# A recurrent attention block with streamed weights: new homes for two residual tiles, a larger GpSimd descriptor ring, and a smaller kept part of one output unit

## The chip, the cores and the metric

The kernel runs on one core of one Trainium2 chip. The metric is the device time of that core in microseconds (us), the median of the runs shown.

## The reference, cut to what matters

Two blocks are computed from one layer-normed input and added to it. Block B is a dense layer with GELU (1024 to 3584 to 1024). Block A is attention that passes over the sequence in 64 segments of 32 tokens and carries 8 memory rows from each segment to the next, so its segments can't be computed side by side:

```python
xn = _layernorm(x)                                   # x: 1 x 2048 x 1024
mem = mem0                                           # 8 rows
for s in range(64):
    h = concatenate([mem, xn[:, 32*s:32*s+32]])      # 40 rows
    q, k, v = h @ Wq, h @ Wk, h @ Wv                 # 32 heads of 128
    p = softmax(where(mask, q k^T * scale, -1e9))
    o = (p v) @ Wo                                   # 40 x 1024
    mem = o[:, :8]; outs.append(o[:, 8:])
return x + concatenate(outs) + B(xn)
```

## The kernel before

**Two parts.** The first part (about 440 us) computes the layer norm, block B and the residual R = x + B(xn), and writes to DRAM what the loop reads again: for each segment a row of `hr_d` that holds the transposed input (columns 0 to 255) and the residual (columns 256 to 511), and for the rows called left a row of `hrL_d` in the same form. The second part is the loop over 64 segments, `for s in range(NSEG)`, written out in full: there is no loop on the chip. All instructions of an engine run in the order in which the code makes them (`manual_schedule`); a tracker of the written and read regions of each tile adds the semaphore waits.

**Segments in groups of four.** `g, i4 = divmod(s, GRP)`: `i4` is 0 for the first segment of a group, 3 for the fourth. Of the 32 tokens of a segment, 24 are handled in it with the 8 memory rows; the other 8, the left ones, are collected over four segments and pushed through the products once for a group. Which pass carries left rows depends on `i4`: the output product does where `i4 == 1` (and in the last segment), flagged `left_o`. There the sum tile `psX` has 512 columns, 256 of the segment and 256 of the left rows.

**Weight units.** The four weight matrices are 64 units of 128 x 2048 bf16 (512 KB), used in each segment in the order K, Q, K, Q (half of the heads each), V, V, O. 46 units stay in SBUF; 18 are read anew in every segment (`PLACED` marks them with S). Of those, two are kept in PSUM banks and are copied into a slot by VectorE (L242); the others come from DRAM copies `Wc_...` over SyncE's queue (L244, L246) into one of six slots (`STREAM_BUFS`). `unit_done` (L669) runs after each unit's product: it starts the next stream into the slot that has become free, and takes one or two entries of the list `small`, which are DMAs on GpSimd's queue. One streamed output unit, `HALF`, is special: the first of its two 128 x 1024 parts stays in SBUF in `half_home` (L137), and only the second is streamed (L243); `o_product` takes the kept part from `half_home` (L899).

**One segment.** Passes K0, Q0, K1, Q1, V0, V1 multiply the input `hr_home` (line L709) with the units. `scores(0)` runs after the first unit of Q1: products into `mixed`, then the exp of ScalarE from `mixed` into the attention-weight tile `pr_all` (L823), then the masking on VectorE (L828). `sums(0)`, after the last unit of Q1, adds up `pr_all` (L836, L842), makes the reciprocals on ScalarE (L847, L850), and writes the scaled weights to `pd_main` and `pd_left` (L857, L861). `scores(1)` and `sums(1)` do the same in V1. `values` multiplies `pd_main` and `pd_left` with V (L876, L882) and stores to `d_oL` or `b_oL` (L890). Then the O pass (L902) sums 16 units into `psX`, one of three PSUM banks that the passes share. At its end the first rows become the new memory: ScalarE copies `psX` (L997), `put_mem` transposes it on TensorE (L277), and VectorE casts it into `hr_home` (L281), which has been loaded with the next segment's input meanwhile (L254, issued after V1). Last, VectorE adds the residual to `psX` in place of the residual tile (L1012), the bank is let go (L1018), and GpSimd's queue stores the tile.

**Homes of the residual.** The residual of the segment is loaded at the first unit of the O pass by `load_res` (L964) into `pr_all`, which the exps of the segment have finished with. In a `left_o` segment the left residual is loaded after unit 7 of the O pass into the first 256 columns of `pd_main` (L991, L992). The next segment's exp (L823) writes to `pr_all` again.

**Stores.** They go by GpSimd's queue. Where `i4` is 0 or 3, four stores of 24 rows go from `pr_all` straight to the output (L1051). Where `left_o` holds, four stores go to `outL_d` (L1017) and from there, by `small`, to the output (L1042). Where `i4 == 2`, the tile goes to `outM_d` (L1044) and from there by `small` in two pieces of 12 tokens to the output (L1048). In segments 1 to 4 `small` also holds the transfers of the last residual rows from `R_n` to `hr_d` and `hrL_d` (L446).

**The lowest SBUF bytes.** The area of GpSimd's DMA descriptors is cut to `SCRATCH` = 352 bytes per partition (L130), and `SMALL` = 3744 bytes behind it hold `half_home`, `pr_all`, `pd_main`, `hr_home` and some constants at fixed addresses. `ident`, the identity matrix of the first part's transposes, lies in `pr_all`.

The softmax here doesn't subtract the row's maximum and nothing guards it: scores larger than these inputs give would overflow.

## Time and profile before

| | us |
|---|---|
| median of the three runs shown | 1982.02 (1969.82 to 1986.70) |
| the profiled execution, its own time | 1987.94 |
| its span, first to last instruction | 1986.2 |
| TensorE busy (matmuls) | 1747.1, 88% of the span |
| VectorE, ScalarE, GpSimd busy | 918.9, 638.5, 286.6 |
| DMA: bytes moved, mean rate over the span | 610.03 MB, 307 GB/s |
| granted TensorE clock, mean | 0.983 |

All shares and waits are those of the one profiled execution. A busy TensorE means that matmuls are in its pipeline, not that it works at its peak. A row of the waits reads: engine, tile and line that waited, what ended the wait, us in total, how often, the longest. A row of the timeline reads: start in us from the span's start, us, engine, line, operation, what it writes and reads, how many such instructions were merged, and in brackets the idle time before it with what ended it. "issue" there stands for a wait that the profile shows no semaphore for. A row of sums over stretches reads: the stretch, its length, busy us of PE, PEld, DVE, ACT and POOL with the number of instructions, the granted clock, the mean busy share of the 16 DMA engines, and GB/s.

### The profile page before, as it was taken

Reading aid. Unit: us, or ns where it says so; the run is one execution under the profiler, and the core shown is the slowest. Engines: PE = TensorE matmul, PEld = TensorE weight load, DVE = VectorE, ACT = ScalarE, POOL = GpSimd, SP = SyncE. Lnnn points to the kernel's source line nnn. Section 1 sums busy time; section 2 is a strip of 40 time slices with the busy share of each in tenths; the row PEclk is TensorE's granted clock in tenths of the full one; section 3 lists DMA queues with packets and bytes.
Section 4 is the critical chain, followed back from the end, with each engine's and each line's share of the span. In section 5 each row is a group of like instructions: output and inputs, shape, how many; then the busy total and the mean of one; then the engine's idle time right before and its main releaser. Section 6 shows DMA issues by size and latency. Waiting matters only on the chain. (4 is left out here: it accounts for less than half of the span.)

```text
span 1986.2 us, 73232 instructions
## 1 busy us (share of the span) xinstructions
PE 1747.1 (88%) x32275; PEld 938.2 (47%) x32275; DVE 918.9 (46%) x2222; ACT 638.5 (32%) x1356; POOL 286.6 (14%) x554
## 2 busy tenths in 40 slices
PE   7999999987878888998988888888888989888887
PEld 3444444444444454555544545454444445444443
DVE  6656565323434444444444444444444444444443
ACT  6343434212222332333333233233232333223232
POOL 0000000002331111111111121111111111111111
PEclk9999999989899999999999999999999999999999
DMA  9821212888889999999999999999999999899997
GB/s 329 243 55 42 56 41 56 305 321 308 290 317 342 349 360 339 373 368 373 347 376 356 349 374 341 353 362 363 347 356 341 386 357 375 326 358 356 339 359 294
DMA packets 220283, 610.03 MB, mean 307 GB/s; under 512 B 47675, under 2 KB 65771, under 8 KB 219948
## 3 DMA queue, kind: packets, MB, share of 16 engines
q1 hardware_dynamic: 199036, 585.18, 80.0%
q0 software_dynamic: 16832, 17.52, 2.8%
q8 instruction: 253, 4.15, 0.8%
q10 hardware_dynamic: 4096, 2.64, 0.4%
q14 instruction: 66, 0.54, 0.1%
HBM read 591.00 MB, written 30.21 MB: 313 GB/s over the span
## 5 line engine op out<-in xcount | busy, mean ns | idle before, releaser
L709 PE MATMUL acc<-u,hr_home 128*32 128x512 bf16 x11520 | 791.8, 387 | 60.7 <-DVE hr_home L281 21.3
L709 PEld LDWEIGHTS <-hr_home 128*32 128x32 bf16 x12288 | 345.6, 98 | 360.3 <-issue 62.4
L709 PE MATMUL acc<-u,hrL 128*32 128x512 bf16 x2880 | 256.4, 389 | 22.4 <-issue 8.2
L498 PE MATMUL ps<-u 128*128 128x512 bf16 x896 | 195.6, 381 | 2.6 <-ACT u L382 2.6
L902 PE MATMUL acc<-u,d_oL 128*32 128x256 bf16 (+1 forms) x3330 | 173.2, 290 | 18.8 <-DMA u<-Wc_O 15.9
L242 DVE COPY u<-kept 128x1024 bf16<-128x1024 bf16 x254 | 163.0, 683 | 16.0 <-PE acc L902 7.2
L902 PEld LDWEIGHTS <-b_oL 128*32 128x32 bf16 (+1 forms) x3552 | 108.9, 99 | 86.4 <-issue 50.0
L902 PE MATMUL acc<-u,b_oL 128*32 128x256 bf16 (+1 forms) x1776 | 119.0, 291 | 31.9 <-DMA u<-Wc_O 24.3
L547 PE MATMUL ps<-u 128*128 128x512 bf16 x672 | 147.0, 379 | 0.0
L498 PEld LDWEIGHTS <-u 128*128 128x128 bf16 x896 | 88.0, 98 | 108.9 <-issue 3.4
L902 PEld LDWEIGHTS <-d_oL 128*32 128x32 bf16 (+1 forms) x3552 | 104.4, 98 | 68.5 <-issue 28.2
L857 DVE TENSOR_TENSOR pd_main<-pr_all,mixed 128x320 bf16<-128x320 bf16 x128 | 61.9, 484 | 143.6 <-ACT mixed L850 141.5
L709 PEld LDWEIGHTS <-hrL 128*32 128x32 bf16 x3072 | 85.4, 97 | 86.5 <-issue 24.5
L767 DVE STREAM_TRANSPOSE b_oL<-b_oL 128x512 bf16<-128x512 bf16 x128 | 90.5, 707 | 63.4 <-ACT b_oL L753 63.4
L828 DVE TENSOR_TENSOR pr_all<-pr_all,mixed 128x96 bf16<-128x96 bf16 (+1 forms) x256 | 37.9, 189 | 166.1 <-ACT pr_all L823 166.1
L753 ACT CAST kT<-acc 128x512 bf16<-128x512 f32 x64 | 37.5, 585 | 237.2 <-PE acc L709 237.2
L902 PE MATMUL acc<-W_O,b_oL 128*32 128x256 bf16 (+1 forms) x1776 | 106.2, 289 | 6.1 <-issue 6.1
L753 ACT CAST b_oL<-acc 128x512 bf16<-128x512 f32 x128 | 75.2, 587 | 109.9 <-PE acc L709 109.9
L254 POOL DMA_DIRECT2D hr_home<-hr_d x58 | 33.1, 571 | 488.8 <-PE acc L709 394.0
L547 PEld LDWEIGHTS <-u 128*128 128x128 bf16 x672 | 65.3, 98 | 77.4 <-DVE g_u L514 0.4
L281 DVE CAST hr_home<-mixed 128x64 bf16<-128x64 f32 x63 | 14.1, 225 | 186.6 <-PE mixed L277 120.1
L997 ACT CAST d_oL<-acc 128x256 bf16<-128x256 f32 (+1 forms) x63 | 26.8, 426 | 221.3 <-PE acc L902 221.3
(132 smaller groups left out, 2120.7 us busy)
## 6 DMA issues: line engine op xcount, KB each, us to landing
u<-Wc_K SPq DMA_DIRECT2D x256, 512.0 KB
u<-Wc_V SPq DMA_DIRECT2D x256, 512.0 KB
u<-Wc_O SPq DMA_DIRECT2D x256, 512.0 KB
u<-Wc_Q SPq DMA_DIRECT2D x192, 512.0 KB
u<-Wc_O SPq DMA_DIRECT2D x64, 256.0 KB
u<-in_B_w_dram SPq DMA_DIRECT2D x14, 512.0 KB
u<-in_A_Wq_dram SPq DMA_DIRECT2D x13, 512.0 KB
u<-in_A_Wv_dram SPq DMA_DIRECT2D x12, 512.0 KB
```

The lines of the kernel that those rows point to most:

```text
L242: nc.vector.tensor_copy(out=t[:, c0:c0 + 1024], in_=bank)
L254: eng.dma_start(out=hr_home[:, :], in_=hr_d[s, :, 0:256])
L281: nc.vector.tensor_copy(out=hT[:, :, NX:SEG].rearrange("p (j c) t -> p j c t", c=nc_), in_=psM.rearrange("p c j t -> p j c t"),)
L498: nc.tensor.matmul(ps[:, :].rearrange("p (s t) -> p s t", t=SEG), lhsT=w1_sb[fb // 14 * 8 + kt][:, (fb % 14) * P:(fb % 14 + 1) * P], rhs=x ...
L547: nc.tensor.matmul(ps[:, :], lhsT=gts[fc // 4][:, fc % 4, t * P:(t + 1) * P], rhs=w2_sb[fc // 2][:, fc % 2, cs], start=(fc == 0), stop=(fc ...
L709: nc.tensor.matmul(o, lhsT=lhs[:, i, :], rhs=m, start=(i == seq[0]), stop=(i == seq[-1]), tile_position=(0, 32 * j),)
L753: cp(out=out, in_=ps.rearrange("p (h e) -> p h e", e=32))
L767: nc.vector.transpose(out=home, in_=home)
L828: nc.vector.tensor_tensor(out=p, in0=p, in1=m[:, None, :].to_broadcast([P, 4, n]), op=ALU.min)
L857: nc.vector.tensor_tensor(out=pdA.rearrange("p c b q -> p b c q"), in0=prA[:, None, :, :].to_broadcast([P, 2, 4, 40]), in1=dd, op=ALU.mult,)
L902: nc.tensor.matmul(acc[r:r + n // 8, 0:n], lhsT=lhs[:, 4 * (i % 4) + 2 * u + k, :], rhs=w_k[:, n * jq:n * jq + n], start=(unit == O_UNITS[ ...
L997: nc.scalar.copy(out=o_sb[:, 0:no, :], in_=psX[:, 0:32 * no].rearrange("p (h e) -> p h e", e=32))
```

## The change

- The descriptor area grows from 352 to 512 bytes per partition; the area of small tiles behind it shrinks by as much.
- Of the special output unit, now called `PART`, 512 of its 2048 columns stay in SBUF (`part_home`, the first quarter of the old `half_home`), and 1536 are streamed in each segment instead of 1024.
- The freed half of `half_home` holds two tiles of 256 columns: `res_home` for the segment's residual, and `pr_all`. The place of the old `pr_all` goes to `hr_home`; `pd_left` moves from a pool to a fixed address; `ident` lies in `pd_main`.
- `load_res` fills `res_home` instead of `pr_all`. The left residual is loaded into `pr_all`, after unit 1 of the O pass instead of after unit 7 into `pd_main`.
- In a `left_o` segment, the left residual is added and stored first, and then the segment's own.
- Where `i4 == 2`, the output leaves `outM_d` in one DMA of 24 tokens instead of two of 12.

```diff
-SCRATCH = 352
-SMALL = 3744
+SCRATCH = 512
+SMALL = 3584
...
-AT_BANKS, AT_HALF = 5, 2
+AT_BANKS, AT_PART = 5, 2
+PART_COLS = 512
...
     half_home = nc.alloc_sbuf_tensor_at("half_home", [P, DM], BF16, offset=SCRATCH)
-    pr_all = nc.alloc_sbuf_tensor_at("pr_all", [P, 256], BF16, offset=SCRATCH + 2048)
+    hr_home = nc.alloc_sbuf_tensor_at("hr_home", [P, 256], BF16, offset=SCRATCH + 2048)
     pd_main = nc.alloc_sbuf_tensor_at("pd_main", [P, 320], BF16, offset=SCRATCH + 2560)
-    hr_home = nc.alloc_sbuf_tensor_at("hr_home", [P, 256], BF16, offset=SCRATCH + 3200)
-    small_consts = nc.alloc_sbuf_tensor_at("small_consts", [P, 16], BF16, offset=SCRATCH + 3712)
+    pd_left = nc.alloc_sbuf_tensor_at("pd_left", [P, 128], BF16, offset=SCRATCH + 3200)
+    small_consts = nc.alloc_sbuf_tensor_at("small_consts", [P, 16], BF16, offset=SCRATCH + 3456)
+
+    part_home, res_home, pr_all = half_home[:, 0:PART_COLS], half_home[:, 512:768], half_home[:, 768:1024]
...
-        elif unit == HALF:
-            nc.sync.dma_start(out=t[:, 1024:2048], in_=copies[unit])
+        elif unit == PART:
+            nc.sync.dma_start(out=t[:, PART_COLS:], in_=copies[unit])
...
-                    w_k = half_home if unit == HALF and k == 0 else t[:, 1024 * k:1024 * k + 1024]
                     for jq in range(DM // n):
-                        r = n // 8 * jq
+                        r, c0 = n // 8 * jq, DM * k + n * jq
+                        w_t = part_home if unit == PART and c0 < PART_COLS else t
...
-                            rhs=w_k[:, n * jq:n * jq + n],
+                            rhs=w_t[:, c0:c0 + n],
...
             def load_res():
-                st["res"] = pr_all
+                st["res"] = res_home
...
-                if n == 7 and left_o:
-                    st["resL"] = pd_main[:, 0:256]
+                if n == 1 and left_o:
+                    st["resL"] = pr_all
                     nc.gpsimd.dma_start(out=st["resL"][:, :], in_=hrL_d[og, :, 256:512])
...
-            for w, r in enumerate(tiles):
+            for w, r in reversed(list(enumerate(tiles))):
...
-                for t in (slice(0, NX // 2), slice(NX // 2, NX)):
-                    small.append(lambda o=o[:, t, :], r=r[:, t, :]: nc.gpsimd.dma_start(out=o, in_=r))
+                small.append(lambda o=o, r=r: nc.gpsimd.dma_start(out=o, in_=r))
```

## The prediction, made before the changed kernel ran

> **What bounds the kernel now.** I read four views in this order: the slices of the page, the waits of TensorE, the GpSimd queue and a timeline of one segment, and sums over stretches.

> Slices first. From slice 9 of 40 on (about 447 us) the recurrent loop runs, and the DMA engines are 8 or 9 tenths busy until the end. They carry the streamed weights.

> ```profile
> DMA  9821212888889999999999999999999999899997
> GB/s 329 243 55 42 56 41 56 305 321 308 290 317 342 349 360 339 373 368 373 347 376 356 349 374 341 353 362 363 347 356 341 386 357 375 326 358 356 339 359 294
> ```

> Sums over stretches (us, busy of PE, PEld, DVE, ACT, POOL, granted clock, DMA share, GB/s) say how near the loop is to that limit:

> ```profile
> 549.00:580.00 31.00, 22.56 (x514) 12.89 (x517) 10.68 (x25) 7.35 (x17) 14.76 (x27) 0.89 0.78 280
> 604.00:1960.00 1356.00, 1176.05 (x26960) 663.16 (x26952) 604.97 (x1438) 419.67 (x969) 224.39 (x418) 0.99 0.96 357
> 1380.80:1408.60 27.80, 24.89 (x606) 15.31 (x600) 12.24 (x29) 7.66 (x19) 3.00 (x5) 1.00 1.01 385
> 1408.60:1431.00 22.40, 18.23 (x448) 10.11 (x449) 10.65 (x25) 6.98 (x16) 3.15 (x6) 1.00 0.85 297
> ```

> Over the steady part the DMA engines are 0.96 busy at 357 GB/s, so 0.04 x 1356 = 54 us are idle DMA time. The same view laid over single segments (from one memory update at L281 to the next, averaged) puts the idle part where TensorE stalls: share 0.90 in first segments of a group of four, 0.97 in third, 0.99 in second and fourth. The loop is thus nearly stream-bound, with holes that stalls of TensorE tear: a stalled TensorE frees no slot, and with six slots the stream soon has nowhere to write.

> The waits of TensorE (us, times, longest):

> ```profile
> PE acc L902 <- DMA u<-Wc_O: 40.3, 58, 2.6
> PE mixed L836 <- DVE pr_all L828: 30.8, 22, 7.3
> PE acc L709 <- DVE hr_home L281: 21.3, 16, 3.2
> PE acc L709 <- DVE pd_main L1012: 19.9, 13, 4.8
> PE acc L709 <- DVE pr_all L1012: 4.0, 5, 1.3
> ```

> The first is the stream itself. The other four, 76.0 us, have causes that the change touches. The GpSimd queue and the timeline at the end of a fourth segment show the causes:

> ```profile
> 1386.48 0.54 POOL L1044 DMA_DIRECT2D outM_d<-pr_all  x1 [6.17 <-DVE pr_all L1012]
> 1391.78 0.66 POOL L1048 DMA_DIRECT2D out_dram<-outM_d  x1 [4.76 <-DMA outM_d<-pr_all]
> 1399.07 0.64 POOL L1048 DMA_DIRECT2D out_dram<-outM_d  x1 [6.63 <-issue]
> 1404.77 0.60 POOL L254 DMA_DIRECT2D hr_home<-hr_d  x1 [5.06 <-DVE b_oL L890]
> 1405.37 0.56 POOL L964 DMA_DIRECT2D pr_all<-hr_d  x1
> 1408.56 0.22 DVE L281 CAST hr_home<-mixed 128x64 bf16<-128x64 f32 x1 [2.95 <-DMA hr_home<-hr_d]
> 1411.39 2.77 PE L709 MATMUL acc<-u,hr_home 128*32 128x512 bf16 x48 [0.64 <-DVE pr_all L1012]
> 1418.56 0.36 ACT L823 ACTIVATE pr_all<-mixed 128x224 bf16<-128x224 f32 x1 [2.62 <-DMA out_dram<-pr_all]
> 1419.30 0.25 PE L836 MATMUL mixed<-pr_all,small_consts 128*32 128x160 bf16 x4 [1.87 <-DVE pr_all L828]
> ```

> The second out piece waits 6.63 us on nothing that has a semaphore, and starts 0.3 us after the first has landed (1398.77); the load of hr_home starts 0.3 us after the second has landed (1404.47). V's products ended near 1400.4, so the load is some 4 us late, with it the memory update, the residual, its stores, and the next exp, which writes into pr_all while the stores still read it.

> [...]

> **The change part by part.** Sums are against the profiled execution, 1987.94 us (span 1986.2 and 1.7 around it); the median shown is 5.9 us lower.

> *Own residual home (L962).* The exp of L823 no longer waits for stores of the main residual: its waits for out_dram<-pr_all and outM_d<-pr_all, 38.2 + 7.3 us, end, and with them TensorE's 30.8 us at L836. The timeline has 13.3 of these at 533, 564 and 590 us (4.6, 7.3, 1.4), 17.5 later. The load of L964 also stops waiting for L861 (37.5 us, 38 times: about 1.0 us earlier each), worth the 4.0 us of L1012 pr_all. Next late is the exp's own input, mixed L817.

> *Left residual in pr_all, loaded at unit 1 (L991) and added first (L1011).* Today it waits for pd_main, which the value products read to unit 6, and L1012 waits 41.2 us in 16 segments for it to land; TensorE loses 19.9 us because the bank psX stays taken. At unit 1 it waits only for L861, done before, is issued some 4 us earlier and lands (4.9 us) as the output products end. All 19.9 us go. It adds a wait: in the 16 segments that follow, the exp waits for the two stores of the left half. In the group at 1362, L281 is at 1362.16, these stores would land near 1368 by the 4.3 and 4.7 us of their like, and the exp is due near 1368.7. Behind the exp stand the rest of ACT's work and L836. Bounds: 0, and 16 x 0.7 = 11 us should they land as late as the slowest 7 us of this queue; I take 1.

> [...] the second piece's issue and its wait go (91.8 us in 16, off the path). A load still has to wait for that piece [...]. Its landing is not in the trace: between 7.0 us (the first piece; latency hides the rows) and 11.4 (two of 5.7). From 1391.8 that frees the load at 1399 to 1403.5, against 1404.8, and V's end at 1400.4 is what it then waits for. Of the 21.3 us at L281 the timeline has 17.8 at these ends; I take 15 (bounds 5 and 17.8).

> *A quarter kept (L54, L243, L899).* 128 KB more per segment, 64 times 0.131 MB = 8.4 MB. At a full stream, 357/0.96 = 371 GB/s, that is 0.353 us x 64 = 22.6 us. The product reads its weights from another address; instruction and shape counts don't change. The copy in the first part is two DMAs for one, in slices with DMA 1 to 2 tenths busy: nothing. ident and pd_left move house: nothing.

> *The sum.* Removable stalls: before 604 us, 13.3 + 4.8 (pd_main, at 497) + 0.9 = 19; after, 17.5 + 15 + 15.1 + 3.1 - 1 = 50. They don't all become time, because TensorE would only meet the stream sooner. Before 604 the DMA share in the three slow segments is 0.78 to 0.84, so I let 75% through: 14. After, the ceiling is the 54 us of idle DMA; the holes lie where the stalls are, which speaks for most, and the stream's wait (40.3 at L902, in the same segments) for less: 65%, 33 (choice; bounds 20% and 100%: 10 and 50). The added bytes at 0.96 of 22.6: 22. Net -14 - 33 + 22 = -25: 1963 for the profiled execution, **1957** from the median.

> **The rivals.** *The stream takes it back* (slower than before). Slots are freed sooner, but the stream has no more to give: 20% of the 50 us come through, 10, early ones 4 [...], and the bytes cost all 22.6: +9, 1991; at no conversion 2005. For it: 0.96 busy, and TensorE waits for Wc_O just where the added quarter is streamed. Against it: a share of 0.85 at 297 GB/s in the segment after the late load. It decides once less than 22.6/69 = 33% of the stalls convert. *The single piece holds the queue as long as two did*: 15 less to gain, 10 of it time: -15, 1967; [...] against it: 5.7 us is mostly latency, as these pieces land in 2.2 when the DMA is quiet. *Everything converts*: 19 + 50 - 22 = -47, 1935, as second and fourth segments run today at 0.99.

> **How the numbers follow.** Chances: forecast 0.43, stream takes it back 0.22, single piece 0.18, everything converts 0.17. About 1% is what a measurement of this kernel can tell from no change (its runs shown span 0.85%): 1962 and 2002. Faster by more: most of the forecast and all of the last, 0.53; slower by more: the far end of the stream rival, 0.10; the rest 0.37. The range, 1930 to 1997, leaves out 0.1 on either side.

> **What would show it.** Right: no wait of L823 on an out store; hr_home's load in every fourth segment at V's end; one out piece of about 7 to 9 us; L1012 not waiting for hrL_d; DMA share near 0.98 in first segments; L836, L281 and L1012 gone from TensorE's waits, Wc_O's wait grown by less than they were. Wrong: Wc_O's and the other streams' waits grown by as much as the others shrank at a share that stays 0.96; exp waiting for outL_d<-pr_all in third segments.

## The result: 1911.98 us, and the profile after

The changed kernel takes 1911.98 us (median of four runs, 1909.69 to 1917.95). The kernel before, measured beside it, takes 1984.36 us (four runs, 1969.82 to 1989.31). The ratio is 0.965, with a 95% interval from 0.960 to 0.971. So the change is 72 us faster. The forecast was 25 us faster, 1957 us, in a range from 1930 to 1997: the sign was right, the size was not, and the measured time lies 18 us below the range.

Everything below compares one profiled execution of each kernel: spans of 1986.2 and 1911.5 us, 74.7 us apart. Line numbers of the loop are 5 higher in the changed kernel (L281 is now L286, L709 is L714, L836 is L841, L902 is L907, L1012 is L1017), those of the last output stores 4 higher (L1048 is L1052). The tracker names `res_home` and `pr_all` by the tile that they are parts of, `half_home`.

**The slices of the page**, after. Columns are 40 equal parts of the span: the granted TensorE clock in tenths, the DMA share in tenths, GB/s.

```profile
PEclk9999999998999999999999999999999999999999
DMA  9921212598999999999999999999999999999998
GB/s 339 259 53 42 57 43 53 208 330 301 392 378 388 373 381 384 384 367 396 373 389 376 363 377 362 353 376 382 376 393 383 386 364 379 356 388 365 380 373 318
```

The DMA row was 8 or 9 through the loop and is now 9 from the eleventh slice to the last but one, with 353 to 396 GB/s. And there is a row that the prediction did not show. Before, it had a second dip inside the loop:

```profile
PEclk9999999989899999999999999999999999999999
```

The digit 8 that both kernels have is a stretch of 10.2 us at half clock, from 432 us before and from 431 after, where the first part passes into the loop. The other 8 of before, in the slice from 497 to 546 us, is gone.

**Sums over stretches.** The columns are the stretch, its length, busy us of PE, PEld, DVE, ACT and POOL, the granted clock, the DMA share, GB/s. Both ends of a stretch are starts of the cast of the new memory (L281, L286), so that the same segments are compared: first segments 1 to 4, called early, then the 58 after them, called later. Before:

```profile
468.10:579.40 111.30, 88.47 (x1908) 47.67 (x1900) 42.28 (x101) 29.41 (x68) 41.81 (x76) 0.91 0.85 306
579.40:1957.70 1378.30, 1195.46 (x27348) 672.86 (x27344) 613.66 (x1459) 427.24 (x986) 227.61 (x424) 0.99 0.96 357
```

After:

```profile
466.81:558.54 91.73, 81.53 (x1908) 48.00 (x1900) 42.70 (x101) 29.45 (x68) 41.38 (x75) 1.00 1.00 383
558.54:1884.40 1325.86, 1186.46 (x27348) 677.87 (x27344) 615.61 (x1459) 426.87 (x986) 219.27 (x410) 1.00 0.99 377
```

The four early segments give 19.6 us, the 58 later ones 52.4 us; the rest of the 74.7 us, 2.7, lies outside. Two readings of these rows matter:

- TensorE executes the same 27348 matmuls in the later stretch and is busy 9.0 us less; in the early stretch, with 1908 matmuls in both, 6.9 us less. A wait that goes away cannot do that. A higher clock can, and the rows show one: 0.91 and 0.99 before, 1.00 after.
- The stream moves more bytes in less time. Later stretch: 492 MB at 357 GB/s, then 499 MB at 377.

**The waits of TensorE**, after, over the whole span (us, times, longest):

```profile
PE acc L714 <- issue: 30.6, 36, 2.0
PE acc L907 <- DMA u<-Wc_O: 28.4, 57, 1.6
PE acc L907 <- issue: 20.6, 25, 2.6
PE mixed L816 <- DVE b_oL L772: 19.1, 31, 0.7
...
PE acc L714 <- DVE hr_home L286: 2.4, 6, 0.7
...
PE acc L714 <- DVE half_home L1017: 0.2, 1, 0.2
```

The four waits that the prediction set out to remove were 76.0 us. L836 (now L841) on the masking and L1012 (now L1017) on `pd_main` are no longer in the list (two issue waits, 2.6 us together, are left at L841), the one on `hr_home` is 2.4 us, the one on the residual 0.2 us. The stream's own wait, Wc_O, did not grow; it fell from 40.3 to 28.4 us. What grew is "issue", the wait without a semaphore.

**What TensorE's issue waits are.** The page lists a DMA queue of the kind "instruction":

```profile
q8 instruction: 252, 4.13, 0.8%
```

These are 252 packets of 16 KB. In the later stretch TensorE has 40 issue waits before and 72 after. Each of them ends 1.2 to 1.6 us after the end of a packet of this queue; only 6 to 7% of all matmuls start at such a distance. And when TensorE's instructions are counted off in blocks of 256, all these waits come at the same place of a block, to within two instructions. I read them as waits for its next block of instructions; the traces show the packets and the places, not what is in them. One such wait cuts a run of 12 products in two:

```profile
1653.07 0.81 PE L714 MATMUL acc<-u,hrL 128*32 128x512 bf16 x9
1655.91 0.40 PE L714 MATMUL acc<-u,hrL 128*32 128x512 bf16 x3 [2.03 <-issue]
```

In the later stretch these waits grow from 32.3 to 62.1 us, while those on the stream's DMAs fall from 44.5 to 35.6. On that reading, the changed kernel waits longer for instructions than for the stream.

**GpSimd's queue** in one group, after (start, us, engine, line, what it writes and reads, in brackets the idle time before it and what ended it):

```profile
1338.26 0.55 POOL L1049 DMA_DIRECT2D outM_d<-half_home  x1 [6.75 <-DVE half_home L1017]
1343.55 0.71 POOL L1052 DMA_DIRECT2D out_dram<-outM_d  x1 [4.74 <-DMA outM_d<-half_home]
1353.44 0.57 POOL L259 DMA_DIRECT2D hr_home<-hr_d  x1 [9.19 <-PE acc L714]
1354.01 0.54 POOL L969 DMA_DIRECT2D half_home<-hr_d  x1
1360.45 2.05 POOL L1055 DMA_DIRECT2D out_dram<-half_home  x4 [5.90 <-DVE half_home L1017]
```

One out piece, and the load of `hr_home` behind it is released by TensorE (the end of V); before, the second piece had waited 6.63 us at the issue ahead of it. The whole queue: 56 of the 58 loads at L259 are released by the products at L714, the other two by those at L907.

### The profile page after: what moved, and what is told of

The parts are those of the page before. It is cut to its first block, busy times and chain, and to the rows that moved or that the text cites. A ratio compares the mean times of both kernels' runs of the same rounds, so it can differ in the third digit from the quotient of the medians.

```text
span 1911.5 us, 72993 instructions
## 1 busy us (share of the span) xinstructions
PE 1728.4 (90%) x32255; PEld 943.5 (49%) x32275; DVE 921.1 (48%) x2222; ACT 638.3 (33%) x1356; POOL 277.3 (15%) x538
## 3 DMA queue, kind: packets, MB, share of 16 engines
q10 hardware_dynamic: 4096, 2.64, 0.5%
## 4 chain that ended last, share of the span: by engine, by line
PE 67%; DMA 20%; DVE 6%; issue 4%; ACT 3%; POOL 0%; DVEq 0%; ACTq 0%; POOLq 0%; SPq 0%
PE acc L714 32%; DMA u<-Wc_O 14%; PE ps L503 10%; PE acc L907 10%; PE ps L552 8%; DMA u<-Wc_Q 2%; PE ps L587 2%; PE acc L881 2%; ACT mixed L855 1%; DVE b_oL L772 1%; PE mixed L816 1%; DMA hr_home<-hr_d 1%; DVE pd_main L862 1%; PE pT L587 1%; ACT mixed L852 1%
## 5 line engine op out<-in xcount | busy, mean ns | idle before, releaser
L714 PE MATMUL acc<-u,hr_home 128*32 128x512 bf16 x11520 | 777.8, 381 | 27.4 <-issue 12.3
L714 PEld LDWEIGHTS <-hr_home 128*32 128x32 bf16 x12288 | 350.5, 97 | 309.6 <-issue 62.1
L714 PE MATMUL acc<-u,hrL 128*32 128x512 bf16 x2880 | 256.3, 380 | 22.2 <-issue 14.3
L907 PE MATMUL acc<-u,d_oL 128*32 128x256 bf16 x3441 | 181.5, 292 | 21.0 <-DMA u<-Wc_O 12.5
L907 PEld LDWEIGHTS <-b_oL 128*32 128x32 bf16 (+1 forms) x3552 | 109.4, 98 | 84.8 <-issue 49.5
L907 PEld LDWEIGHTS <-d_oL 128*32 128x32 bf16 (+1 forms) x3552 | 107.5, 99 | 74.1 <-issue 37.0
L907 PE MATMUL acc<-u,b_oL 128*32 128x256 bf16 (+1 forms) x1776 | 118.7, 290 | 26.8 <-DMA u<-Wc_O 15.9
L862 DVE TENSOR_TENSOR pd_main<-half_home,mixed 128x320 bf16<-128x320 bf16 x128 | 62.5, 488 | 155.5 <-ACT mixed L855 144.8
L714 PEld LDWEIGHTS <-hrL 128*32 128x32 bf16 x3072 | 86.8, 96 | 81.5 <-issue 25.3
L907 PE MATMUL acc<-W_O,b_oL 128*32 128x256 bf16 (+1 forms) x1776 | 106.4, 289 | 8.1 <-issue 8.1
L259 POOL DMA_DIRECT2D hr_home<-hr_d x58 | 32.7, 564 | 554.2 <-PE acc L714 546.9
L758 ACT CAST kT<-acc 128x512 bf16<-128x512 f32 x64 | 37.5, 586 | 220.2 <-PE acc L714 220.2
L855 ACT ACTIVATE mixed<-mixed,small_consts 128x160 f32<-128x160 f32 x256 | 94.2, 368 | 8.4
L511 ACT ACTIVATE g_xb<-ps,b1col 128x512 bf16<-128x512 f32 x112 | 76.9, 687 | 60.1 <-PE ps L503 59.0
```

Of the source, the lines that this page charges most:

```text
L511: nc.scalar.activation(out=xb[:, :], in_=ps[:, :], func=ACT.Identity, bias=b1col[:, fb:fb + 1], scale=1.0)
L714: nc.tensor.matmul(o, lhsT=lhs[:, i, :], rhs=m, start=(i == seq[0]), stop=(i == seq[-1]), tile_position=(0, 32 * j),)
L758: cp(out=out, in_=ps.rearrange("p (h e) -> p h e", e=32))
L855: nc.scalar.activation(out=mixed[:, 160 * b:160 * b + 160], in_=mixed[:, 0:160], func=ACT.Exp, scale=-1.0, bias=off[:, b:b + 1],)
L862: nc.vector.tensor_tensor(out=pdA.rearrange("p c b q -> p b c q"), in0=prA[:, None, :, :].to_broadcast([P, 2, 4, 40]), in1=dd, op=ALU.mult,)
L907: nc.tensor.matmul(acc[r:r + n // 8, 0:n], lhsT=lhs[:, 4 * (i % 4) + 2 * u + k, :], rhs=w_t[:, c0:c0 + n], start=(unit == O_UNITS[0] and k ...
```

## The experiments: two set out, none measured; and what the two traces tell apart

No variant of either kernel was measured for this study. So no run separates the homes from the descriptors, and none prices the added bytes alone. Two experiments with expectations on record were to divide the change into its parts; they are shown because they say which question is left open, and how it can be settled. Their expectations were written after the two traces had been read. Two more were set out with expectations and not measured either: the added bytes alone in the kernel before, and the changed kernel with 128 KB less per segment. In the two expectations below, theory A holds that waits and the half clock behind them both turn into time; theory C is the forecast's: waits alone, at two thirds.

*The larger descriptor area and the single piece alone*, with the changed kernel's bytes, against the changed kernel:

```diff
-                st["res"] = res_home
+                st["res"] = pr_all
...
-                if n == 1 and left_o:
-                    st["resL"] = pr_all
+                if n == 7 and left_o:
+                    st["resL"] = pd_main[:, 0:256]
...
-            for w, r in reversed(list(enumerate(tiles))):
+            for w, r in enumerate(tiles):
```

> [...] the homes of the residual as before. Theory A (waits, and half clock behind them, go with the homes and with the queue): 1952 to 1972 us, ratio 0.984 to 0.994; the waits on L836 and pd_main stay. Theory C (waits alone, at two thirds, as forecast): about 1942 us is reached only with the homes, here no gain over 1 per cent.

Measured: nothing; no chip ran it.

*The homes alone*, with the changed kernel's bytes and a small descriptor area (320 bytes; before had 352), against the changed kernel:

```diff
-SCRATCH = 512
-SMALL = 3584
+SCRATCH = 320
+SMALL = 3776
...
-                small.append(lambda o=o, r=r: nc.gpsimd.dma_start(out=o, in_=r))
+                for t in (slice(0, NX // 2), slice(NX // 2, NX)):
+                    small.append(lambda o=o[:, t, :], r=r[:, t, :]: nc.gpsimd.dma_start(out=o, in_=r))
```

> Edit: only the two homes of the change, with its bytes; the out pieces stay two [...]. Theory A: 1937 to 1947 us, ratio 0.976 to 0.981, with fewer than 8 half-clock stretches in the loop; hr_home's waits stay. Theory C: 1950 to 1965 us.

Measured: nothing; no chip ran it. Theory A and theory C thus stand untested by a run, and the division between the parts, which both give in numbers, is not shown.

What follows is argued from two traces; where it says "behind" it means order in time, not a shown cause. Two comparisons inside the traces come nearest to an experiment.

**First comparison: the four segments of a group.** The change touches different waits in each place of a group, while the added quarter is streamed in all of them. Averages over the later stretch, us per segment (14 or 15 segments of a place), from cast to cast; a wait counts where it ends. "Named" is the sum of TensorE's waits on an instruction of another engine. Each cell has before, then after.

| place | length | named waits | waits on DMAs | issue waits | TensorE busy |
|---|---|---|---|---|---|
| first | 23.60, 22.98 | 2.49, 0.18 | 1.03, 0.26 | 0.45, 2.15 | 20.55, 20.32 |
| second | 24.08, 24.12 | 1.88, 0.74 | 0.23, 0.35 | 0.30, 0.90 | 21.73, 22.05 |
| third | 22.67, 21.60 | 1.82, 0.83 | 1.63, 1.63 | 0.34, 0.29 | 18.71, 18.73 |
| fourth | 24.76, 22.74 | 0.82, 0.82 | 0.15, 0.16 | 1.17, 1.00 | 21.51, 20.73 |

The fourth and the first have to be read together, since the late load of `hr_home` lengthens the end of the fourth, and the wait for it ends in the first. Three readings:

- Fourth and first: 2.31 us of named waits go, 0.76 of DMA waits go too, 1.53 of issue waits come, TensorE is busy 1.01 us less, and the pair is 2.64 us shorter.
- Second: 1.14 us of named waits go, 0.60 of issue waits and 0.12 of DMA waits come, TensorE is busy 0.32 us longer, and the length does not change. This place ran at a DMA share of 0.99 before and does so after. The rival "the stream takes it back" gives the right length here, but TensorE's own waits on the stream hardly grow. Whether the full DMA engines or the issue waits hold the length is not shown.
- Third: 0.99 us of named waits go (those on `pd_main` were 1.01), the others stay, the segment is 1.07 us shorter. All of it converts, and TensorE's waits show no sign of the added bytes.

Times the number of segments: 14 x 2.64 = 37 from the pair, 15 x 1.07 = 16 from the third, nothing from the second: 53, which is the later stretch's gain. The homes' and the descriptors' waits mix in the pair (0.59 us of L836 and 1.27 of `hr_home` in the first place), so this does not divide the gain between the two parts of the change.

**Second comparison: the clock, stretch by stretch.** The trace's clock record has 14 stretches inside before's loop at half the granted clock, 58 us together: three of 6.8 us among the early segments, eleven of 3.4 us later. After has three of 3.4 us, 10 us together. Two of before's, in the columns of the sums above:

```profile
497.00:504.00 7.00, 6.15 (x60) 2.28 (x64) 3.06 (x6) 0.58 (x1) 3.75 (x8) 0.52 0.44 123
562.00:569.00 7.00, 4.03 (x48) 1.56 (x52) 3.50 (x9) 1.90 (x5) 5.97 (x11) 0.53 0.25 76
```

In the first of them, TensorE is busy 6.15 of 7 us and gets through 60 matmuls; after has 160 in 6.14 busy us at about the same time of the loop:

```profile
497.00:504.00 7.00, 6.14 (x160) 3.35 (x156) 4.45 (x13) 3.34 (x9) 4.33 (x8) 1.00 1.00 387
```

(The mixes of matmuls differ, so 60 to 160 is no ratio of clocks.) Each of before's stretches was laid beside the waits ahead of it. Nine start in or just behind a wait that the change removes or shortens: at 497 and 610 us behind `pd_main` (4.8 and 2.2 us), at 531, 562 and 1705 behind L836 (4.6, 7.3, 2.7), at 753, 1125, 1221 and 1507 behind `hr_home` (3.2, 2.1, 2.5, 2.9). The other five stand behind one wait on issue or several shorter waits, most of them on issue or on the stream. The timeline of TensorE at 1507 us of before (start, us, operation, idle time before it in brackets) shows one:

```profile
1503.59 0.82 PE L709 MATMUL acc<-u,hrL 128*32 128x512 bf16 x12
1507.26 0.62 PE L709 MATMUL acc<-u,hr_home 128*32 128x512 bf16 x4 [2.86 <-DVE hr_home L281]
1507.66 1.50 PE L709 MATMUL acc<-low,hr_home 128*32 128x512 bf16 x12
1508.94 3.42 PE L709 MATMUL acc<-u,hr_home 128*32 128x512 bf16 x44
```

Ahead of the wait, 12 products take 0.82 us; behind it, 12 products of the same shape and line take 1.50 us, in the stretch recorded at half clock. The end of the stretch at 562 us shows the way back, in the same view:

```profile
567.03 0.64 PE L709 MATMUL acc<-u,hr_home 128*32 128x512 bf16 x4
567.45 0.64 PE L709 MATMUL acc<-u,hrL 128*32 128x512 bf16 x4
...
569.12 0.39 PE L709 MATMUL acc<-u,hr_home 128*32 128x512 bf16 x4
569.34 0.38 PE L709 MATMUL acc<-u,hrL 128*32 128x512 bf16 x4
```

Four products begin every 0.43 us up to 568.3 us, and every 0.22 us from 568.7 us, just behind the end of the half in the clock record (568.63). Nothing is waited for between them, so this is the clock and not a stall. The length of a wait does not tell which waits half clock follows: one of 2.11 us at 1122 us was followed by it, and one of 2.60 at 674 us was not.

A better sign can be worked out from the clock record. In each trace all its changes inside the loop lie a whole number of 3.413 us apart (from 561.80 to 1507.30 us it is 277 times). So each loop can be cut into windows of that length, with every change at an edge. The two waits in such windows:

```profile
674.43:677.84 3.41, 1.64 (x52) 1.11 (x55) 0.04 (x1) 0.37 (x1) 0.00 (x0) 1.00 1.01 381
1121.59:1125.00 3.41, 1.30 (x28) 0.49 (x26) 0.52 (x2) 0.00 (x0) 0.00 (x0) 1.00 0.98 371
```

The longer wait is cut by an edge, and TensorE is busy for 0.48 of the worse window. The shorter one lies in one window and leaves 0.38 of it. The loops of the two kernels have 854 such windows at full clock. In 12 of them TensorE is busy for less than 0.40 of the window, and half clock follows all 12. Between 0.40 and 0.45 it follows 4 of 10, above 0.45 it follows 1 of 832. In these two traces half clock thus goes with the busy share of such a window, below about 0.4, and not with the length of one wait. That the share is its cause is not shown.

What such stretches cost can be read in two ways. The sums over before's 13 stretches in the compared segments, and over after's 3:

```profile
sum 54.61, PE 47.76 PEld 21.50 DVE 22.29 ACT 8.81 POOL 20.53; mean PE 3.67 PEld 1.65 DVE 1.71 ACT 0.68 POOL 1.58
sum 10.24, PE 10.24 PEld 5.67 DVE 2.87 ACT 3.22 POOL 1.93; mean PE 3.41 PEld 1.89 DVE 0.96 ACT 1.07 POOL 0.64
```

Four products begin every 0.43 us at half clock and every 0.22 us behind it (at 568 us of before). An estimate from that: half of the busy time is lost, 23.9 us before, 5.1 after, 18.8 apart. By the busy rows, TensorE is 6.9 + 9.0 = 16 us less busy for the same loop. So the second gain is 16 to 19 us. Whether it costs the stream as well is not shown: in these stretches the DMA share is anything from 0.18 (1507 us) to 1.03 (958 us), and the waits ahead of them may leave the slots full too.

## Why the prediction was wrong

**What held.** The steps named as signs of a right forecast came out: the exp no longer waits on an output store of the main residual, the load of `hr_home` is released at V's end, L1017 does not wait for the load of the left residual, the three waits have gone but for 2.6 us, the DMA share of first segments is 0.98.

- *Own residual home*: sized at 30.8 us of waits at L836 and 4.0 at L1012; measured 30.8 and 3.8 gone. Right.
- *Left residual at unit 1*: 19.9 us said to go, 19.9 gone. The added wait of the exp for the left half's stores was taken as 1 us (bounds 0 and 11). Measured, ScalarE's wait: 

```profile
ACT half_home L828 <- DMA outL_d<-half_home: 1.2, 3, 0.5
```

  Three times, 0.5 us at the longest. Right.
- *The larger descriptor area and one out piece*: 15 of 21.3 us were expected to go, 18.9 went, with all parts of the change in place. The landing of the single piece, bounded at 7.0 and 11.4 us, is 5.3 at the least, 6.2 in the middle and 7.1 at the most, about the lower bound or below it. So the lower bound was the right one and the rival "single piece holds the queue" was wrong; 24 rows took 0.5 us more than 12 had (5.7). That the queue had waited for room in the descriptor area was the author's estimate: the trace of before shows a wait of 6.63 us that ends 0.3 us behind a landing, not what it waited for.

**What failed.** The step "They don't all become time, because TensorE would only meet the stream sooner", with 75% of the early stalls and 65% of the later, and 22 us for the bytes on top. Here are its terms, TensorE's time against what the two traces have (early: segments 1 to 4; later: the 58 after them):

| term | forecast | measured |
|---|---|---|
| early, idle time of TensorE | -14 (19 x 75%) | -12.6 (22.8 to 10.2) |
| early, busy time of TensorE | none | -6.9 |
| later, the stalls named | -50 | -56.7 |
| later, named waits not listed (kL 5.7, rest 1.9) | none | -7.6 |
| later, waits on the stream, bytes among it | +17 and +22 | -8.9 |
| later, issue waits (read as instructions) | none | +29.8 |
| later, busy time of TensorE | none | -9.0 |
| sum | -25 | -72 |

The rows of the later stretch come from its waits: `hr_home` fell from 21.0 us to 2.1, L836 from 18.9 to 0, `pd_main` from 15.1 to 0, L1012 from 4.0 to 0.2; all named waits from 101.9 to 37.6, those on DMAs from 44.5 to 35.6; issue grew from 32.3 to 62.1.

So TensorE did not meet the stream sooner: it waited for the stream 9 us less, with 7 MB more streamed. What grew instead were the issue waits, read above as waits for instructions, which the prediction had no term for. Of the 47 us between -25 and -72, the largest share is this giving back: 39 us were charged, and 21 came on balance, 18 too much. The half clock behind waits had no term: 16 us. The stalls themselves were sized too small by 7, and those at kL and others, which the sum did not list, are 7.6 more; the early idle time was 1.4 too large. 18 + 16 + 7 + 7.6 - 1.4 = 47. That 21 came back where 22 had been set for the bytes alone is chance, since it came as another wait.

**Where the ceiling went wrong.** The later stalls' conversion was capped by "the ceiling is the 54 us of idle DMA", 0.04 of the stretch. Its accounting can be redone for both traces from the packets, with more digits: share times length is busy DMA time.

- Before, 1378.3 = 1325.4 busy + 52.9 idle, at 371.3 GB/s while busy.
- After, 1325.9 = 1317.7 busy + 8.2 idle, at 379.0 GB/s while busy.

Idle DMA fell by 44.7 us, within the ceiling. The added 7.2 MB cost 19.5 us at the old rate, as charged. But busy DMA time carried 2% more bytes in each us, which is 27 us. The share counts a DMA engine as busy while its packets are slow, so a share of 0.96 is no proof that 0.96 of the stream's best rate is used. Most packets of the stream are of 4096 bytes; their median time is 159 ns in both kernels, but 2.1% of them took over 400 ns before and 1.7% after, and together they took 23 us less of the 16 engines' time. The wider rows of the special unit's new copy, another possible reason, give about 3 us: its 7424 packets of 3072 bytes took 123 ns each, where those of 2048 bytes had taken 87, which is 130 ns for as many bytes. 385 GB/s in one stretch was among the lines of the prediction, over the 371 that the ceiling rested on; the rate was there to be seen. Why fewer packets are slow when TensorE stalls less is open: no run here tells fuller queues from fewer small transfers in their way.

**And the half clock was on the page.** The prediction showed a stretch with a granted clock of 0.89, beside the mean of 0.983 for the whole run, and took neither into the sum. With the long waits went this second cost, 16 to 19 us in all. The rival "Everything converts" (1935) came nearest, and was still 23 us short, mostly for want of this term.

**The rival on the other side**, "The stream takes it back", decided from a conversion below 33%. Over the loop it was wrong; in the second segments of a group, which had been at a share of 0.99, its length came true, though not by waits on the stream.

**What stays open.** How the 72 us divide between the homes and the descriptors; how much of the half clock would remain with one of the two alone; what moved the stream's rate while busy; why there are more issue waits, and whether they are waits for instructions; whether these waits cost time of their own, or stand where TensorE would have waited for weights. The two experiments above would settle the first two. The one with 128 KB less per segment would say whether the stream still bounds the changed kernel.

## What to carry to other kernels

When a kernel nearly runs at its stream's limit, size that limit by the best rate in a busy stretch and by segments side by side, not by the DMA share, which calls slow packets busy (0.96 at 357 GB/s here, beside a stretch at 385). Before costing a stall, cut the trace into windows of 3.41 us from a change of the granted clock: where TensorE was busy for less than 0.40 of one, half clock followed here, 12 times of 12, a second cost behind the wait that shows as busy time (16 to 19 us). When TensorE's "issue" waits are large, lay them beside the packets of the instruction queue before putting them down to the stream: here each ended 1.2 to 1.6 us behind one. And an issue wait on GpSimd's queue that ended 0.3 us after an earlier DMA's landing (6.63 us) was gone here with a larger descriptor area and one piece less; which of the two did it is not shown, as no run changed the area alone.
